# Sliding-window attention scores: five sets of exponentials per group in place of six, with quarter blocks in 32x64 tiles

## The chip, the cores and the metric

The kernel runs on one core of a Trainium2 chip. The metric is the device time of one launch in microseconds (us). A NeuronCore has a matrix engine (TensorE, called PE in the profile; its weight loads are listed apart as PEld), a vector engine (VectorE, DVE), a scalar engine (ScalarE, ACT), a general engine (GpSimd, POOL) and a queue engine for transfers (SyncE, SP). Each works through its own list of instructions in order, and they meet by semaphores. TensorE writes to PSUM; all other data here lie in SBUF.

## The reference, cut to what matters

One transformer block on a sequence of 2048 tokens with 640 channels, in bfloat16:

```python
mod = (_silu(c) @ w_mod).reshape(c.shape[0], 6, 1, -1)      # sa, ca, ga, sb, cb, gb
h = _layernorm(x) * (1 + ca) + sa
x = x + ga * attention(h, A_wqkv, A_wo)                     # 32 heads of 20 channels, window 256
h = _layernorm(x) * (1 + cb) + sb
x = x + gb * ((sigmoid(h @ w_gate) * (h @ w_up)) @ w_down)  # 640 -> 1536 -> 640
```

In the attention a query at position i sees the keys from i - 255 to i:

```python
mask = (idx[:, None] - idx[None, :] >= 0) & (idx[:, None] - idx[None, :] < W)   # W = 256
scores = jnp.where(mask, q @ k^T * Dh ** (-0.5), -1e9);  o = softmax(scores) @ v
```

## The kernel before

**Chunks, groups, blocks.** The 2048 tokens go in eight chunks `a` of 256 queries, two blocks of 128 each. For a chunk the kernel does a layer norm, transposes it, projects Q, K and V, turns Q and K so that channels lie on partitions (by transposing DMAs from the staging tile `stg`, except for chunk 0), does the attention, the output projection, the second layer norm and the gated MLP. The 32 heads form eight groups of four: heads with the same `gi` lie on partitions 0, 32, 64 and 96 (20 of 32 used), and `j` counts these four. The attention of a chunk goes in two halves `q`, each with four `gi` (called `k` in the code); such a pair (chunk, half) is called a group below.

**Scores.** A query block of a chunk touches the key blocks at the offsets -2, -1 and 0 (first block) or -1, 0 and 1 (second block), counted in blocks from the chunk's first. Per head that makes six blocks of 128 keys by 128 queries: four of them are cut by a diagonal of the window (offset -2 with the first query block, -1 with the second, 0 with the first, 1 with the second), and of each of these four one half is dead. `plan` (L931) lays these blocks in sets. A set fills one score tile `S`, four PSUM banks with 512 columns each, one bank for each `j`. The tile pool for `S` has one tile, so a set's matmuls wait until the exponential of the set before has read it. A main set holds the blocks of offsets 0 and -1 of one `k` (8 matmuls of 256 columns); an edge set holds the blocks of offsets -2 and 1 of two `k` (16 matmuls of 128 columns). A group has four main and two edge sets; chunk 0, with no keys before it, has three sets in each half. That makes 14 x 6 + 2 x 3 = 90 sets.

**A set's course.** `score_set` (L945) issues the matmuls (through `mm`, L626, with a tile position: each of the four `j` uses its own 32 rows of the array and all 128 columns), then one exponential on ScalarE from `S` to a tile `E` (L975; 128 x 2048 elements), then masks on POOL that set the dead half of each cut block to zero (`affine_select`, L983 and L985): in a main set two of 512 elements per partition, in an edge set two of 1024. There are eight `E` tiles.

**Products with V.** `burst` (L992) multiplies all `E` of a group with V: 64 matmuls, each on 32 columns of the array (`j` picks which), 32 of 256 and 32 of 128 columns. From chunk 1 on it is held in `pend` and put in front of the matmuls of the next group's second set, in one operation of TensorE. V has a column of ones, so that the sums of the softmax come out beside the products; `norm` divides (VectorE).

**Order.** Nothing is ordered at run time. `A(...)` records operations with the tiles they read and write, and `PLAN` is a written list of them all in the order of issue; an entry is five times the operation's number plus the engine's. `SLOTS` is a written list of the buffers that tiles take. `schedule` turns both into one list for each engine, and `emit` puts in the semaphore waits that the tiles call for. Between score sets the list of TensorE holds matmuls of projections and of the MLP (through the same `mm`, L625).

## Time and profile before

| what | value |
|---|---|
| time, median of 3 runs | 329.41 us (328.96 to 330.71) |
| profiled execution, first to last instruction of the program (span) | 327.1 us |
| profiled execution, time with what surrounds the program | not on the page; the median lies 2.3 us above the span |
| PE busy | 318.7 us, 97% of the span |
| ACT busy | 231.4 us, 71% |
| DVE busy | 196.7 us, 60% |
| POOL busy | 183.0 us, 56% |
| 90 exponentials (L975) | 169.0 us of ACT |
| masks (L983, L985) | 139.3 us of POOL |

Busy time is the union of an engine's instructions. A matmul's record reaches from its issue to a modelled end, so records of matmuls overlap, and the time that one costs is read from start to start. In a timeline row the first number is the start, the second how long the merged row lasts, then engine, line, operation, what it writes and reads, the shapes (stationary rows*columns, then moving rows x columns) and how many instructions the row merges. In a row of waits stand the total in us, the number of times and the longest.

### The profile page before, as it was taken

What the parts mean: (1) busy time and instruction counts of PE and PEld (TensorE: products, weight loads), DVE (VectorE), ACT (ScalarE), POOL (GpSimd) and SP (SyncE); (2) the same over time, 40 slices, a digit from 0 to 9 for tenths busy, and PEclk for the clock granted to TensorE, in tenths of its full rate; (3) what the DMA queues carried; (4) which work ended last, traced back from release to release, by engine and by line L of the source; (5) the groups of instructions that cost most, each with busy time, mean ns of one, the idle gap of its engine ahead of it and who ended that gap; (6) DMA issues with size and microseconds to landing.
All of it is one profiled execution on the core that took longest, in us unless ns stands there. A gap on an engine that the chain in (4) does not pass through costs nothing.

```text
span 327.1 us, 9812 instructions
## 1 busy us (share of the span) xinstructions
PE 318.7 (97%) x4123; PEld 227.8 (70%) x4123; DVE 196.7 (60%) x422; ACT 231.4 (71%) x227; POOL 183.0 (56%) x279
## 2 busy tenths in 40 slices
PE   5999899999999999999999999999999999999997
PEld 2666556567776777665767667766777777788885
DVE  6796799678485545675457554456727463484333
ACT  2489799987787898879797968785897568322120
POOL 4248579789688563778383745646490837402000
DMA  7989899999902281321802100360051012202101
GB/s 231 373 319 196 178 271 192 222 289 274 218 18 40 42 139 34 82 42 44 170 0 44 32 2 19 80 125 2 1 82 42 2 42 43 82 0 42 40 2 40
DMA packets 64613, 33.52 MB, mean 102 GB/s; under 512 B 49082, under 2 KB 63034, under 8 KB 64570
## 3 DMA queue, kind: packets, MB, share of 16 engines
q1 hardware_dynamic: 63200, 31.27, 42.2%
q10 hardware_dynamic: 1370, 1.64, 1.5%
q8 instruction: 32, 0.52, 0.7%
q14 instruction: 11, 0.09, 0.1%
HBM read 18.35 MB, written 2.62 MB: 64 GB/s over the span
## 4 chain that ended last, share of the span: by engine, by line
PE 93%; DMA 3%; DVE 1%; ACT 1%; issue 0%; POOL 0%; SPq 0%; DVEq 0%
PE M L625 77%; PE S L626 9%; PE M L626 7%; DMA QT<-stg 1%; DMA x<-in_A_x_dram 1%; ACT E L975 1%; DVE st L732 1%; DVE x L753 0%; SPq L524 0%; POOL st L740 0%; ACT QT L655 0%; DVE hT L814 0%; DVE st L734 0%; DVE x L1159 0%; POOL st L738 0%
## 5 line engine op out<-in xcount | busy, mean ns | idle before, releaser
L975 ACT ACTIVATE E<-S 128x2048 bf16<-128x2048 f32 x90 | 169.0, 1877 | 36.3 <-PE S L626 34.4
L983 POOL TENSOR_SCALAR_AFFINE_SELECT E<-E 128x512 bf16<-128x512 bf16 (+2 forms) x90 | 73.7, 830 | 36.2 <-ACT E L975 15.1
L985 POOL TENSOR_SCALAR_AFFINE_SELECT E<-E 128x512 bf16<-128x512 bf16 (+1 forms) x84 | 65.6, 790 | 36.4 <-ACT E L975 30.7
L625 PE MATMUL M<-h2T,wu 128*128 128x256 bf16 x480 | 73.6, 273 | 0.0
L625 PE MATMUL M<-h2T,wg 128*128 128x256 bf16 x480 | 72.7, 273 | 0.0
L1140 DVE SCALAR_TENSOR_TENSOR hh<-sig,M 128x512 bf16<-128x512 f32 x48 | 32.4, 681 | 49.5 <-ACT sig L1138 27.2
L625 PE MATMUL M<-wd,hh 128*128 128x320 bf16 (+2 forms) x396 | 60.5, 295 | 0.0
L625 PEld LDWEIGHTS M<-h2T,wu 128*128 128x128 bf16 x480 | 45.1, 98 | 10.8 <-issue 2.7
L1138 ACT ACTIVATE sig<-M 128x512 f32<-128x512 f32 x48 | 28.5, 596 | 33.5 <-PE M L625 32.4
L625 PEld LDWEIGHTS M<-h2T,wg 128*128 128x128 bf16 x480 | 45.2, 98 | 9.9 <-issue 1.9
L625 PEld LDWEIGHTS M<-wd,hh 128*128 128x128 bf16 x396 | 36.8, 98 | 14.9 <-issue 1.9
L626 PE MATMUL S<-QT,KT 20*128 20x256 bf16 (+1 forms) x960 | 35.9, 245 | 1.8 <-DMA QT<-stg 1.3
L626 PEld LDWEIGHTS S<-QT,KT 20*128 20x128 bf16 x960 | 14.1, 92 | 21.9 <-ACT E L975 11.6
L732 DVE BATCH_NORM_STATS2 st<-x 128x6 f32<-128x320 bf16 x64 | 29.0, 476 | 0.6 <-DMA x<-in_A_x_dram 0.5
L625 PE MATMUL M<-wk,hT 128*128 128x320 bf16 x160 | 29.4, 300 | 0.0
L1021 DVE STREAM_TRANSPOSE T<-M 128x512 f32<-128x512 f32 x32 | 21.6, 698 | 12.7 <-PE S L626 12.2
L625 PE MATMUL M<-wv,hT 128*128 128x320 bf16 x160 | 28.6, 300 | 0.0
L625 PE MATMUL M<-wo,oT 128*128 128x320 bf16 x160 | 28.0, 300 | 0.0
L625 PE MATMUL M<-wq,hT 128*128 128x320 bf16 x160 | 27.6, 300 | 0.3 <-DVE hT L814 0.3
L1159 DVE TENSOR_TENSOR x<-M,x 128x320 bf16<-128x320 f32 (+2 forms) x33 | 15.4, 475 | 17.9 <-PE M L625 17.6
L1094 DVE TENSOR_TENSOR x<-M,x 128x320 bf16<-128x320 f32 x32 | 15.3, 486 | 16.0 <-PE M L625 15.3
L656 DVE CAST stg<-M 128x320 bf16<-128x320 f32 x33 | 15.7, 483 | 12.5 <-PE M L625 12.4
(82 smaller groups left out, 303.2 us busy)
## 6 DMA issues: line engine op xcount, KB each, us to landing
x<-in_A_x_dram SPq DMA_DIRECT2D x10, 320.0 KB, 4.3
wd<-in_w_mod_dram SPq DMA_DIRECT2D x6, 320.0 KB, 5.1
wd<-in_B_w_down_dram SPq DMA_DIRECT2D x4, 480.0 KB, 5.0
out_dram<-x SPq DMA_DIRECT2D x4, 320.0 KB, 2.4
wg<-in_B_w_gate_dram SPq DMA_DIRECT2D x2, 576.0 KB, 7.3
wu<-in_B_w_up_dram SPq DMA_DIRECT2D x2, 576.0 KB, 5.9
wu<-in_w_mod_dram SPq DMA_DIRECT2D x1, 960.0 KB, 11.0
out_dram<-x ACTq DMA_DIRECT2D x3, 320.0 KB, 2.3
```

The costliest lines, as they stand in the source:

```text
L625: return e.matmul(o, l, r, start=st, stop=sp, skip_group_check=True)
L626: return e.matmul(o, l, r, start=st, stop=sp, tile_position=tp, skip_group_check=True)
L656: return e.tensor_copy(dst(), src())
L732: A("dve", lambda e, g, bi=bi, j=j: e.bn_stats(v(bi * 12 + j * 6, 6), src[bi].ap[:, j * 320:(j + 1) * 320]), 0.48, reads=[src[bi].r()], wr ...
L975: A("act", lambda e, eng: e.activation(E.ap[:], Sp.ap[:], ACT.Exp, scale=SM_SCALE), 1.876, reads=[Sp.r()], writes=[E.r()], prio=3, tag=f"e ...
L983: return e.affine_select(ap, ap, pattern=[[0, ap.shape[1]], [1, 128]], compare_op=ALU.is_ge, fill=0.0, base=0, channel_multiplier=-1)
L985: return e.affine_select(ap, ap, pattern=[[0, ap.shape[1]], [-1, 128]], compare_op=ALU.is_ge, fill=0.0, base=-1, channel_multiplier=1)
L1021: A("dve", lambda e, g, h=h: e.transpose(T1.ap[:, 512 * h:512 * h + 512], X[h].ap), 0.694, reads=[X[h].r()], writes=[T1.r(h)], prio=3.5, t ...
L1094: A("dve", lambda e, g, ps=ps, bi=bi, half=half: e.tensor_tensor(x1[bi].ap[:, half * 320:half * 320 + 320], ps.ap[:, 0:320], x1[bi].ap[:, ...
L1138: A("act", lambda e, g, pg=pg, sg=sg: e.activation(sg.ap[:], pg.ap[:], ACT.Tanh, scale=0.5), c_act(512), reads=[pg.r()], writes=[sg.r()], ...
L1140: A("dve", lambda e, g, pu=pu, sg=sg, f0=f0: e.scalar_tensor_tensor(out=hh.ap[:, f0:f0 + 2, :], in0=sg.ap[:].rearrange("p (a b) -> p a b", ...
L1159: A("dve", lambda e, g, ps=ps, bi=bi, c0=c0, n=n: e.tensor_tensor(x1[bi].ap[:, c0:c0 + n], ps.ap[:, 0:n], x1[bi].ap[:, c0:c0 + n], op=ALU. ...
```

## The change

The dead half of a cut block of 128 x 128 has one quarter of 64 x 64 that is dead as a whole. A cut block thus has one dead quarter, one live quarter, and two quarters cut by the diagonal. After the change the places of the two dead quarters of a main set are filled with live quarters from the blocks of offset 1 and -2 of the same `k`; what is left of these two blocks goes, 64 queries each, to one edge set per group for all four `k`. So a group has four main sets and one edge set: 14 x 5 + 2 x 3 = 76.

- A main set (`main_set`) now has 24 matmuls. Each writes 64 of the score tile's partitions, so a tile of the array is 32 rows by 64 columns, and the moving parts are 64, 64, 192, 192, 256 and 256 columns, alternating between the two halves of the partitions.
- The edge set (`edge_set`) has 32 matmuls of 64 columns on tiles of 32 rows by 128 columns. Its exponential writes to a tile `F` (4 x 4 x 256 elements per partition) with gaps in the middle of each row; two masks of 1024 elements follow.
- `spread` takes, for each main set, the two foreign quarters out of `E`, masks them and writes them to the gaps in `F` (two `affine_select` of 256 elements), and then masks the places that they leave in `E` with the block around them (two of 512). It runs once both the main set and `F` are there: for the first two main sets after the edge set, which is third of five (`ESI`), for the other two after their own exponential.
- The product with V reads the blocks of offset -1 and 0 from `E` and those of -2 and 1 from `F`: the same 64 matmuls.
- Q's layout puts the two query blocks of a head side by side (`p_QT`), so that a matmul can take any stretch of the 256 queries; the transposing DMAs write to strided rows.
- There are six `E` tiles and one `F` for the eight `E` of before. `PLAN` and `SLOTS` are written anew, for all engines.

```diff
 PLAN = [
...
+NE = 6
+NF = 1
+ESI = 2
...
-    p_QT = sbpool("QT", 3, [128, 2, NG, 128])
+    p_QT = sbpool("QT", 3, [128, NG, 2, 128])
...
-    Eall = sb("E", [128, 8, 2048])
-    p_E = Pool("E", [Eall[:, i, :].rearrange("p (j c) -> p j c", j=4) for i in range(8)])
+    Eall = sb("E", [128, NE, 2048])
+    p_E = Pool("E", [Eall[:, i, :].rearrange("p (j c) -> p j c", j=4) for i in range(NE)])
+    p_F = sbpool("F", NF, [128, 4, 4, 256])
...
+    def turned_heads(key, dst, bi):
+        return dst.ap[:, :, bi, :] if key == "q" else dst.ap[:, bi, :, :]
...
+    def queries(a, gi, c0, n):
+        return lambda j: QT[a].ap[32 * j:32 * j + DH, gi, :, :].rearrange("p b c -> p (b c)")[:, c0:c0 + n]
+
+    def select(dst, src, pattern, base, mul):
+        return lambda e, eng: e.affine_select(dst(), src(), pattern=pattern, compare_op=ALU.is_ge, fill=0.0, base=base, channel_multiplier=mul)
+
+    def score_set(a, q, si, tag, prods, low, E, dst, src):
...
+            for k, kb, p0, np_, c0, n, at in prods:
+                gi, kc = 4 * q + k, (2 * a + kb) // 2
+                rhs = queries(a, gi, c0, n)
                 for j in range(4):
-                    ins = mm(e, Sp.ap[:, j, cu * 128:(cu + n) * 128].rearrange("p (n c) -> p n c", c=128), KT[kc].ap[32 * j:32 * j + DH, kb % 2, gi, :],
-                             QT[a].ap[32 * j:32 * j + DH, u:u + n, gi, :], True, True, tp=(32 * j, 0))
+                    ins = mm(e, Sp.ap[p0:p0 + np_, j, at:at + n], KT[kc].ap[32 * j:32 * j + DH, kb % 2, gi, p0:p0 + np_], rhs(j),
+                             True, True, tp=(32 * j, p0))
...
+    def edge_set(a, q, si):
+
+        F = Tile(p_F, f"F{a}_{q}")
+        prods = []
+        for k in range(4):
+            prods += [(k, -2, 0, 128, 0, 64, 128 * k), (k, 1, 0, 128, 192, 64, 128 * k + 64)]
+        cols = lambda c0, t=F: t.ap[:].rearrange("p j k c -> p (j k) c")[:, :, c0:c0 + 64]
+        score_set(a, q, si, "edge", prods, False, F,
+                  lambda: F.ap[:].rearrange("p j k (u c) -> p (j k) u c", c=64)[:, :, 0:4:3, :],
+                  lambda s: s[:].rearrange("p j (k u c) -> p (j k) u c", u=2, c=64))
+        mask(a, 1024, select(lambda: cols(0), lambda: cols(0), [[0, 16], [-1, 64]], -1, 1), [F.r()], [F.r(-2)])
+        mask(a, 1024, select(lambda: cols(192), lambda: cols(192), [[0, 16], [1, 64]], 64, -1), [F.r()], [F.r(1)])
+        return F
+
+    def main_set(a, q, k, si):
+
+        E = Tile(p_E, f"E{a}_{q}_{k}")
+        prods = [(k, 1, 0, 64, 128, 64, 192), (k, -2, 64, 64, 64, 64, 256), (k, -1, 0, 64, 0, 192, 0), (k, 0, 64, 64, 64, 192, 320),
+                 (k, 0, 0, 64, 0, 256, 256), (k, -1, 64, 64, 0, 256, 0)]
+        score_set(a, q, si, "score", prods, True, E, lambda: E.ap[:], lambda s: s[:])
+        return E
+
+    def spread(a, q, k, E, F):
+        mask(a, 256, select(lambda: F.ap[:, :, k, 128:192], lambda: E.ap[:, :, 192:256], [[0, 4], [1, 64]], 0, -1),
+             [E.r()], [F.r((k, 1)), E.r("s1")])
+        mask(a, 256, select(lambda: F.ap[:, :, k, 64:128], lambda: E.ap[:, :, 256:320], [[0, 4], [-1, 64]], -65, 1),
+             [E.r()], [F.r((k, -2)), E.r("s2")])
+        mask(a, 512, select(lambda: E.ap[:, :, 128:256], lambda: E.ap[:, :, 128:256], [[0, 4], [-1, 128]], -1, 1),
+             [E.r(), E.r("s1")], [E.r("d")])
+        mask(a, 512, select(lambda: E.ap[:, :, 256:384], lambda: E.ap[:, :, 256:384], [[0, 4], [1, 128]], 0, -1),
+             [E.r(), E.r("s2")], [E.r("g")])
+
+    def sets(a, q):
+        if a == 0:
+            return first_sets(q)
+        F, Es = None, []
+        for si in range(5):
+            if si == ESI:
+                F = edge_set(a, q, si)
+                done = range(len(Es))
+            else:
+                Es.append(main_set(a, q, len(Es), si))
+                done = [len(Es) - 1] if F is not None else []
+            for k in done:
+                spread(a, q, k, Es[k], F)
...
+            out.append((k, -1, 0, 2, lambda j, E=E: E.ap[:, j, 0:256], rs))
+            out.append((k, 0, 0, 2, lambda j, E=E: E.ap[:, j, 256:512], rs))
+        for k in range(4):
+            out.append((k, -2, 0, 1, lambda j, k=k: F.ap[:, j, k, 0:128], [F.r(), F.r(-2), F.r((k, -2))]))
+            out.append((k, 1, 1, 1, lambda j, k=k: F.ap[:, j, k, 128:256], [F.r(), F.r(1), F.r((k, 1))]))
+        return out
```

135 lines of the change are left out of this document (59 added, 76 removed), and 214 rows, old and new, of the table PLAN.

## The prediction, made before the changed kernel was run

> **What bounds the kernel now.** I read the first part of the page and the chain that ended last, then the busy time by stretches, then who waited for whom, then the timeline around single score sets.
>
> ```profile
> span 327.1 us, 9812 instructions
> ...
> PE 318.7 (97%) x4123; PEld 227.8 (70%) x4123; DVE 196.7 (60%) x422; ACT 231.4 (71%) x227; POOL 183.0 (56%) x279
> ...
> PE 93%; DMA 3%; DVE 1%; ACT 1%; issue 0%; POOL 0%; SPq 0%; DVEq 0%
> ```
>
> ```profile
> 12.00:56.00 44.00, 42.14 (x615) 27.54 (x615) 36.55 (x89) 37.84 (x43) 28.24 (x46) 1.00 1.01 245
> 56.00:140.00 84.00, 84.00 (x1099) 58.83 (x1085) 54.29 (x119) 71.61 (x72) 61.75 (x84) 1.00 0.64 136
> 140.00:285.00 145.00, 144.98 (x1999) 104.48 (x1996) 77.60 (x152) 111.20 (x95) 85.11 (x121) 1.00 0.23 47
> 285.00:327.00 42.00, 39.78 (x356) 32.72 (x344) 19.99 (x38) 7.67 (x13) 2.57 (x5) 1.00 0.10 27
> ```
>
> The first number after each stretch is its length, the second PE's busy time. From 56 to 285 us PE has no hole (228.98 of 229.00); between 12 and 56 us it lacks 1.9 us; the granted clock is 1.00 throughout. A busy PE need not be one that streams, so I take the price of a column from long rows of matmuls:
>
> ```profile
> 275.80 0.40 PE L626 MATMUL S<-QT,KT 20*128 20x256 bf16 x8
> 276.13 2.35 PE L625 MATMUL M<-wd,hh 128*128 128x320 bf16 x16
> 278.41 0.40 PE L626 MATMUL S<-QT,KT 20*128 20x128 bf16 x16
> 278.74 1.80 PE L625 MATMUL M<-wd,hh 128*128 128x320 bf16 x12
> 280.38 0.38 PE L625 MATMUL M<-h2T,wg 128*128 128x256 bf16 x2
> ...
> 281.80 0.82 PE L625 MATMUL M<-h2T,wg 128*128 128x256 bf16 x6
> 282.45 0.82 PE L625 MATMUL M<-h2T,wu 128*128 128x256 bf16 x6
> 283.11 0.60 PE L625 MATMUL M<-h2T,wg 128*128 128x256 bf16 x4
> ```
>
> Start to start, twelve matmuls of 320 columns take 280.38 - 278.74 = 1.64 us, 0.137 us each; twelve of 256 columns take 283.11 - 281.80 = 1.31 us, 0.109 us each. That is 0.43 ns a column for both widths: in a chain the weights are loaded behind the stream. So the kernel is bound by what PE streams, plus a fixed charge at each change between kinds of work.
>
> The charge is read there too. A score set holds PE from its first matmul to that of the next chain: 276.13 - 275.80 = 0.33 us for a main set of 8 matmuls, 278.74 - 278.41 = 0.33 us for an edge set of 16. Each row tile streams 512 columns in it, 2 x 0.109 = 0.22 us; the other 0.11 us is fill and drain. Ahead of it stands another drain: the 16 matmuls from 276.13 should be through at 276.13 + 16 x 0.137 = 278.32, and the set starts at 278.41, 0.09 us later. A set thus costs PE 0.42 us.
>
> Real waits of PE are few:
>
> ```profile
> PEld S L626 <- ACT E L975: 11.6, 46, 0.4
> PEld S L626 <- issue: 8.0, 28, 1.6
> ...
> PE S L626 <- DMA QT<-stg: 1.3, 1, 1.3
> ...
> PEld M L626 <- POOL E L983: 1.2, 4, 0.3
> ```
>
> The first two are idle time of the weight loader, most of it the drains just priced, while PE's matmuls still ran; of PE itself only the 1.3 us for one transposed Q is a hole of size.
>
> **The change, part by part.** *Sets removed.* Seven chunks with two groups each go from six sets to five: 90 to 76, and all 14 that go are edge sets. They stand in PE's unbroken stream, so 14 x 0.42 = 5.9 us go from the path.
>
> *Exponentials removed.* 14 go with them:
>
> ```profile
> L975 ACT ACTIVATE E<-S 128x2048 bf16<-128x2048 f32 x90 | 169.0, 1877 | 36.3 <-PE S L626 34.4 <-POOL E L985 0.7
> ```
>
> 14 x 1.877 = 26.3 us leave ScalarE. I count nothing for it: PE has no hole from 56 us on that a faster ScalarE could close. The bounds are 0 and the 1.9 us that PE lacks before 56 us.
>
> *Main sets in 32x64 tiles.* 56 of them, now 24 matmuls each, in six groups of four (one per row tile): 64, 64, 192, 192, 256, 256 columns, alternating between the two halves of the array's columns. Each half streams 64 + 192 + 256 = 512 columns. If the halves run side by side, 0.33 us stands; if one after the other, 1024 columns take 0.44 + 0.11 = 0.55 us. The trace has four row tiles at once (the score sets) and four column tiles at once (the products with V), never both. The nearest row is the latter, where all four tiles share the array's rows as the two halves would:
>
> ```profile
> 141.19 1.33 PEld L626 LDWEIGHTS M<-E,V 128*32 128x32 bf16 x64 [0.26 <-POOL E L983]
> 141.19 1.50 PE L626 MATMUL M<-E,V 128*32 128x256 bf16 x64
> ...
> 142.63 0.12 PEld L626 LDWEIGHTS S<-QT,KT 20*128 20x128 bf16 x8
> 142.63 0.40 PE L626 MATMUL S<-QT,KT 20*128 20x256 bf16 x8
> ```
>
> From 141.19 to 142.63 is 1.44 us for 32 matmuls of 256 and 32 of 128 columns. Four at once that is 8 x 0.109 + 8 x 0.055 = 1.31 us of stream and 0.13 us of drain; one after the other it would be 5.2 us. So column tiles overlap in full, their 64 weight loads included. The Trainium skill, TensorE: Matmul & The Clock Gate, Part 3, says that a weight load overlaps matmuls in flight only where the row group differs. By that rule the halves of a main set would run in series, and the sum below would be +6.6 us in place of -4.0 (the first rival); this trace disagrees, since the 64 loads above share one row group and end within the 1.44 us.
>
> What the halves do not hide is the weight load at the start, since the first groups are only 64 columns (0.027 us) long. The nearest row is the modulation product, 64 columns against full weights each time:
>
> ```profile
> 7.77 0.45 PE L625 MATMUL S<-silubc,wd 128*128 128x64 bf16 x10
> 8.06 0.59 PE L612 MATMUL S<-E 128*128 128x512 bf16 x2
> ```
>
> Ten take 8.06 - 7.77 = 0.29 us, 0.029 us each, a load with every one; so a load fits behind a 64-column matmul. I allow one uncovered load of 0.03 us and take 0.36 us for a main set, near its lower bound of 0.33 because both nearest rows lie there: 56 x 0.03 = +1.7 us (bounds 0 and 56 x 0.22 = +12.3 us).
>
> *Edge sets.* 14 stay, each now eight groups of 64 columns against full weights: 8 x 0.029 = 0.232 us where 0.218 stood, 14 x 0.014 = +0.2 us.
>
> *Masks.* POOL's rows:
>
> ```profile
> L985 POOL TENSOR_SCALAR_AFFINE_SELECT E<-E 128x512 bf16<-128x512 bf16 x56 | 35.5, 640 | 29.2 <-ACT E L975 24.1 <-DVE x L753 2.5 <-DVE Tn L1025 2.5
> L983 POOL TENSOR_SCALAR_AFFINE_SELECT E<-E 128x512 bf16<-128x512 bf16 x56 | 35.2, 639 | 17.1 <-DVE Tn L1025 8.7 <-DVE wo L1187 3.5 <-ACT E L975 3.2
> ...
> L985 POOL TENSOR_SCALAR_AFFINE_SELECT E<-E 128x1024 bf16<-128x1024 bf16 x28 | 30.5, 1091 | 7.2 <-ACT E L975 6.5 <-ACT stg L655 0.7
> ```
>
> A group had eight masks of 512 and four of 1024 elements: 8 x 0.64 + 4 x 1.09 = 9.5 us. It will have eight of 512, eight of 256 (the same line down to 256 gives 0.41 us) and two of 1024: 10.6 us. POOL gains 14 x 1.1 = 15 us on its 183.0, all beside PE unless PV has to wait for it (a rival below). The product with V has the same 64 matmuls, with half of them from the shared edge tile: no change.
>
> *Layout, buffers, order.* Q's transposes land in strided rows. The cost is taken as zero: they are as many as before and PE waited for one of them once. If that one landed 1 us later, it would cost 1 us; if the order covers it, it gives 1.3 us. Eight exponential buffers become six and one edge tile of the size of two: the next group's two first main sets fit beside four held ones, and the edge tile is wanted only after PV has read it, which PE has passed by then. The new order I cannot cost; it can give back at most PE's 1.9 us, and its losses are the rivals.
>
> **Sum.** -5.9 + 1.7 + 0.2 = -4.0 us on a span of 327.1, so 323.1. The runs' median of 329.41 lies 2.3 us above that span, for what surrounds the program's instructions; I carry it over: 325.4 us.
>
> **The rivals.** *The column halves run in series.* For it: no row has row and column tiles at once. Against it: the PV rows. Price: +12.3 + 0.2 - 5.9 = +6.6 us, 336.0 us, slower. It decides from a main set of 0.33 + 5.7/56 = 0.43 us on.
>
> *The weight loads of 64-column tiles are not hidden.* A load's record lasts 0.097 us (the 19.9 us group below). If the third group had to wait for a whole one behind a 64-column matmul, that is 0.097 - 0.027 = 0.07 us a set more, 56 x 0.07 = 3.9 us in place of my 1.7: -1.8 us, 327.6 us; with the first load uncovered as well, no gain at all.
>
> ```profile
> L626 PEld LDWEIGHTS M<-E,V 128*32 128x32 bf16 x960 | 19.9, 97 | 4.1 <-issue 2.3 <-POOL E L983 1.2 <-POOL E L985 0.3
> ```
>
> The Trainium skill, TensorEngine Tiling (Array Packing), Restrictions and Gotchas, says that column tiling excludes the fast weight load, which speaks for this rival; the 32-column loads of PV, also column tiles, show no such cost, and no run here shows one of 64 columns.
>
> *PV waits for masks.* The edge set is third of five. When its exponential ends, POOL has two masks of 1.09 us, then four per main set for two sets, then two more main sets: 2.2 + 4 x 2.1 = 10.6 us. PV comes four sets later. At the 16.3 us between two PVs shown here,
>
> ```profile
> 141.26 1.43 PE M L626 x64
> ...
> 157.58 1.50 PE M L626 x64
> ```
>
> five sets stand 3.2 us apart, so about 4 x 3.2 - 2.2 = 10.6 us pass: no slack, and POOL has other work. Against it: POOL is 56% busy, and the order may put MLP matmuls before PV. From a wait of 4.0/14 = 0.29 us a group on, the gain is gone; 0.7 us a group is +5.8 us, 335.2 us.
>
> *Instruction fetches.* PE gets 2 x 896 = 1792 instructions more (960 score matmuls become 56 x 24 + 14 x 32 + 64 = 1856, each with its load), bunched in the sets.
>
> ```profile
> q8 instruction: 32, 0.52, 0.7%
> ```
>
> 32 packets against 8246 PE instructions is one per 258, so seven more. At 0.7% of 16 engines' 327.1 us, one takes 1.1 us. If PE stood still for the seven new ones that is 8 us; the 32 old ones left no hole after 56 us. I give that little.
>
> **How the numbers follow.** Forecast (halves overlap, loads mostly hidden): 0.62, its own range 322.0 to 327.5. An order that also closes early holes, down to 321.8: 0.05. Loads uncovered, or masks or fetches taking most of the gain, 327.7 to 331: 0.16. Halves in series: 0.10. Mask or fetch waits beyond the gain: 0.07. A change under 0.5% (1.65 us) can hardly be told from none. Faster 0.67, same 0.16, slower 0.17. The range of 321.8 to 331.5 leaves out the worse part of the slower cases and little below.
>
> **What would show it.** A main set's matmuls to the next chain: 0.34 to 0.40 us if right, 0.55 if the halves run in series. The edge set: 0.34 us. PE without holes from 56 us on, and PE's score line near 76/90 of its share of the chain. ScalarE's exponentials at 76 x 1.88 us. A PV whose loader waits for POOL by more than 0.3 us would show the mask rival; a hole in PE ahead of a score set put down to issue, the fetches. A main set over 0.43 us, or holes in PE over 4 us in sum, would make the forecast wrong.

## The result and the profile after

The changed kernel takes 334.49 us (333.88 to 335.52, 6 runs) against 329.19 (328.08 to 330.71, 6 runs) for the kernel before on the same chip: a ratio of 1.0169, 95% interval 1.0143 to 1.0194. Forecast was 325.4, faster. It is slower by 5.3 us, and lies outside the range of 321.8 to 331.5. Medians and ratios in this document leave out the few executions that lie far above the others of their kernel, one of e3 (403.51 us, at a granted clock of 0.756), one of e16 (334.30) and, beside e16 and e17, one of the kernel before.

The first part of its page, the chain that ended last and the queue of instruction fetches:

```profile
span 333.2 us, 11650 instructions
...
PE 318.2 (96%) x5018; PEld 232.5 (70%) x5019; DVE 208.6 (63%) x433; ACT 206.3 (62%) x212; POOL 198.9 (60%) x353
...
q8 instruction: 39, 0.64, 0.8%
...
PE 81%; DMA 6%; POOL 5%; DVE 4%; issue 2%; ACT 2%; SPq 0%; POOLq 0%; DVEq 0%
```

ScalarE fell by 25.1 us (231.4 to 206.3; 26.3 were worked out). POOL rose by 15.9 (183.0 to 198.9), which looks like the 15 that were worked out, but its rows of masks say otherwise:

```profile
L948 POOL TENSOR_SCALAR_AFFINE_SELECT E<-E 128x512 bf16<-128x512 bf16 x112 | 71.5, 652 | 5.1 <-DVE Tn L1092 1.5 <-DVE x L763 0.3
L948 POOL TENSOR_SCALAR_AFFINE_SELECT F<-E 128x256 bf16<-128x256 bf16 x112 | 47.0, 430 | 34.4 <-ACT E L982 17.8 <-PE S L636 5.0 <-DVE h2T L779 4.3
L948 POOL TENSOR_SCALAR_AFFINE_SELECT F<-F 128x1024 bf16<-128x1024 bf16 x28 | 33.0, 1183 | 18.9 <-ACT F L982 18.6 <-DVE x L763 0.3
```

With chunk 0's (4.6 and 4.0 us) all masks sum to 160.1 us, where the same sum in the kernel before is 140.1: 20 us more. The new order took 4 us of other work off POOL (of the modulations of hT and h2T it does 15 in place of 26). The fetches are 39, seven more, as worked out. What is new is the chain: PE's share went from 93% to 81%, and DMA, POOL, DVE and "issue" took it.

The prices of a set, in the chain of waits (start, length, piece):

```profile
89.73 0.36 PE S L636 x24
90.09 2.10 PE M L635 x17
92.19 0.34 PE S L636 x32
92.53 0.32 PE M L635 x2
```

A main set of 24 matmuls holds PE for 0.36 us and an edge set of 32 for 0.34, as forecast. So the change does what it says: matmul by matmul, start to next start, PE's work between 12 us and the last matmul is 4.0 us less than before (the last matmul ends at 324.78 us before, and 0.96 us up to it are idle by that count; after, it is 330.40 and 10.62; 323.82 - 319.78 = 4.04). The time went into PE's waits, which the view of who waits for whom lists for PE:

```profile
PE M L604 <- POOL ident L543: 2.9, 1, 2.9
PE M L635 <- DVE h2T L779: 1.9, 1, 1.9
PE M L636 <- POOL E L948: 1.8, 2, 0.9
PE M L635 <- DVE x L763: 1.7, 2, 1.2
PE M L635 <- issue: 1.2, 1, 1.2
PE M L635 <- DVE V L666: 0.8, 1, 0.8
PE M L636 <- issue: 0.7, 1, 0.7
```

The first and 1.2 us of the fourth are the start, which the kernel before has too; the other 0.5 us of the fourth stand at 12 us. The others are six waits in the middle, 1.9 + 1.8 + 1.2 + 0.8 + 0.7 = 6.4 us in all, where the kernel before had one of 1.3 us. Busy time by stretches (length, then each engine, the granted clock ahead of the last two numbers) shows a second loss:

```profile
41.00:48.00 7.00, 5.49 (x98) 3.20 (x105) 5.66 (x11) 3.90 (x5) 6.44 (x11) 0.76 0.63 180
...
81.00:89.00 8.00, 6.09 (x82) 4.53 (x74) 6.88 (x12) 4.24 (x7) 7.79 (x11) 0.79 1.12 265
...
96.00:330.00 234.00, 233.02 (x3642) 177.32 (x3641) 138.23 (x273) 137.27 (x132) 128.38 (x225) 1.00 0.22 46
```

In two stretches the granted clock was 0.76 and 0.79, where the kernel before has 1.00. A mean of 0.76 over 7 us is 3.4 us at half clock, and so is 0.79 over 8 us: 1.7 us of work lost in each. This is the execution that was profiled, with a granted clock of 0.990 in the mean; the other five have 0.994 or 0.995, which fits one such stretch, and spans of 332.1 to 333.8 us. From 96 us on PE lacks 0.98 us of 234, and that is a single wait.

The sum closes. The span grew by 333.2 - 327.1 = 6.1 us though the work fell by 4.0, so PE lost 10.1 us more than before. Waits 6.4 less the old 1.3, and half clock 3.4, are 8.5 of them; the rest, 1.6 us, is the 0.5 us at 12 us and stretches too short for the lines above. I use this number, the span less 327.1 plus the 4.0 us of work saved, for every run below and call it **PE's loss**. It comes from single executions, and those of the kernel before alone span 326.4 to 329.2 us on one chip (beside e1), so differences of a microsecond in it mean nothing. The expectations on record count holes matmul by matmul instead (1.0 before, 10.6 after). That count takes 80 short broadcast matmuls, which run four at a time, for series work and so lies some 4 us too low in every kernel alike; only its differences mean anything, and they leave out the first 12 us, in which some runs below lose 1 to 5 us.

What started each wait is seen in the timeline and in the chain. At 41.84 us (timeline of PE, POOL and DVE; idle before in brackets):

```profile
41.84 0.79 PE L636 MATMUL M<-E,V 128*32 128x256 bf16 x28 [0.80 <-POOL E L948]
43.33 0.30 PE L636 MATMUL M<-E,V 128*32 128x128 bf16 x4 [0.71 <-issue]
...
39.77 2.02 POOL L948 TENSOR_SCALAR_AFFINE_SELECT E<-E 128x2048 bf16<-128x2048 bf16 x1
41.74 1.37 POOL L948 TENSOR_SCALAR_AFFINE_SELECT F<-E 128x256 bf16<-128x256 bf16 x2
...
40.04 2.42 DVE L1092 TENSOR_TENSOR Tn<-T,Dr 128x640 bf16<-128x640 f32 x1
```

PV waited 0.80 us for a mask of 2.02 us. That mask is one of chunk 0, and the kernel before has it too (two of 2.00 us); it is its place in the order that is new. In the middle of that PV PE stood 0.71 us for no semaphore at all. Two PE stops of that length within 3 us, and the clock fell to half behind them. Beside the mask DVE's divide took 2.42 us; it ended 0.67 us after the mask (42.46 and 41.79), not far from its mean duration in the kernel before, 0.82 us. The 16 divides of each kernel, before and after (shortest, median and longest in ns):

```profile
L1025 DVE TENSOR_TENSOR Tn<-T,Dr x16: 812/819/826, 37.5 to 286.9; 128x640 bf16<-128x640 f32 x16
L1092 DVE TENSOR_TENSOR Tn<-T,Dr x16: 811/826/2425, 40.0 to 292.8; 128x640 bf16<-128x640 f32 x16
```

In the order of before only one divide runs beside a mask, for 0.07 us; in the changed kernel nine do, and six of them take 1.07 to 2.42 us.

At 83.20 us, in the chain:

```profile
75.68 4.99 DMA h2T<-x
...
80.70 1.28 DVE h2T L779 x2
81.98 0.26 DVE Dr L1090
82.24 0.82 DVE h2T L779 x2
...
83.20 5.10 PE M L635 x30
...
92.85 1.21 issue
94.06 2.13 PE M L635 x18
...
114.94 0.95 POOL E L948
```

A transposing load took 4.99 us, the modulations on DVE behind it came late, PE stood 1.91 us, and the second stretch at half clock followed. At 92.85 PE stood 1.21 us for nothing but its own next instruction. At 121.06 a PV waited 0.95 us for POOL, which had worked on its masks and layer norms without a break of over 0.1 us since 108.30. The sixth wait is 0.79 us at 36.78: DVE's copy of V stood in order behind layer-norm statistics that waited 1.7 us for a load, up to 32.29, and behind what DVE did without a pause from there. So four causes are read from the trace, the late loads from the chain alone and tested by no run: masks 1.8 us, late loads behind which DVE works in order 2.7, instructions 1.9, and half clock behind such stops 3.4.

### The profile page after: what moved, and what is told of

It is laid out like the page before. It is cut to its first block, busy times and chain, and to the rows that moved or that the text cites. A ratio compares the mean times of both kernels' runs of the same rounds, so it can differ in the third digit from the quotient of the medians.

```text
span 333.2 us, 11650 instructions
## 1 busy us (share of the span) xinstructions
PE 318.2 (96%) x5018; PEld 232.5 (70%) x5019; DVE 208.6 (63%) x433; ACT 206.3 (62%) x212; POOL 198.9 (60%) x353
## 4 chain that ended last, share of the span: by engine, by line
PE 81%; DMA 6%; POOL 5%; DVE 4%; issue 2%; ACT 2%; SPq 0%; POOLq 0%; DVEq 0%
PE M L635 66%; PE S L636 7%; PE M L636 7%; DMA x<-in_A_x_dram 3%; POOL E L948 2%; ACT E L982 2%; POOL F L948 2%; DMA h2T<-x 1%; DVE st L742 1%; DMA hT<-x 1%; DVE h2T L779 1%; PE S L635 1%; POOL st L750 0%; DVE x L1155 0%; PE S L622 0%
## 5 line engine op out<-in xcount | busy, mean ns | idle before, releaser
L982 ACT ACTIVATE E<-S 128x2048 bf16<-128x2048 f32 x62 | 116.3, 1876 | 41.4 <-PE S L636 41.0
L948 POOL TENSOR_SCALAR_AFFINE_SELECT E<-E 128x512 bf16<-128x512 bf16 (+1 forms) x118 | 80.1, 692 | 8.7 <-ACT E L982 2.5
L635 PE MATMUL M<-h2T,wg 128*128 128x256 bf16 x480 | 67.3, 277 | 1.9 <-DVE h2T L779 1.9
L948 POOL TENSOR_SCALAR_AFFINE_SELECT F<-E 128x256 bf16<-128x256 bf16 x112 | 47.0, 430 | 34.4 <-ACT E L982 17.8
L635 PE MATMUL M<-h2T,wu 128*128 128x256 bf16 x480 | 66.0, 273 | 1.2 <-issue 1.2
L635 PE MATMUL M<-wd,hh 128*128 128x320 bf16 (+2 forms) x396 | 56.5, 295 | 0.0
L948 POOL TENSOR_SCALAR_AFFINE_SELECT F<-F 128x1024 bf16<-128x1024 bf16 x28 | 33.0, 1183 | 18.9 <-ACT F L982 18.6
L636 PE MATMUL S<-QT,KT 20*64 20x64 bf16 (+5 forms) x1856 | 32.4, 230 | 0.5 <-ACT E L982 0.2
L982 ACT ACTIVATE F<-S 128x2048 bf16<-128x2048 f32 x14 | 26.3, 1877 | 9.0 <-PE S L636 8.8
L636 PEld LDWEIGHTS S<-QT,KT 20*64 20x64 bf16 (+1 forms) x1856 | 15.7, 101 | 18.1 <-ACT E L982 7.9
```

Source lines behind the costliest of these rows:

```text
L635: return e.matmul(o, l, r, start=st, stop=sp, skip_group_check=True)
L636: return e.matmul(o, l, r, start=st, stop=sp, tile_position=tp, skip_group_check=True)
L948: return lambda e, eng: e.affine_select(dst(), src(), pattern=pattern, compare_op=ALU.is_ge, fill=0.0, base=base, channel_multiplier=mul)
L982: A("act", lambda e, eng: e.activation(dst(), src(Sp.ap), ACT.Exp, scale=SM_SCALE), 1.876, reads=[Sp.r()], writes=[E.r()], prio=3, tag=f"e ...
```

## The experiments

First four questions: which cause, then whether the sets or the order carry it.

### e1: the changed sets in the order of before

The changed sets keep the places that the sets of before had, the second edge set of each group goes, and the masks stand where the old ones stood.

```diff
 PLAN = [
-    67, 72, 53, 58, 13, 43, ...
+    76, 139, 89, 63, 84, 202, ...
...
```

> The changed kernel's sets in the order of the kernel before: every operation that both kernels have stands where it stood, the fourth group of operations that a group lost (its second edge set) is left out, and the masks of the one edge set and of the first two main sets stand where those of the first edge set stood. Order theory (the sets save the 4.0 us that the prediction counts, and the new order loses 9.7 us in holes of PE): no hole over 1.5 us after 12 us, the time 4 us below the kernel before, about 325.2 us. Rival (the sets' own waits, masks through one edge tile, lose it in any order): PV waits for POOL in many groups and the time is 330 us or more.

355.02 us (354.40 to 356.70), ratio 1.0788 (1.0750 to 1.0825). The waits of PE:

```profile
PE M L632 <- POOL E L944: 9.5, 7, 2.1
PE M L631 <- issue: 4.3, 2, 2.3
```

PE's loss is 29.9 us (span 353.0). The order theory missed by 30 us, and the mark of its rival was met (330 us or more, PV waiting for POOL). In an order made for other masks, the masks alone cost more than the whole saving. The old order as it stands is no home for the new sets; it says nothing yet on whether a good one exists.

### e2: idle matmuls in the two long waits

```diff
...
+    fill(314, "O0_0x", 3)
+    fill(379, "g", 8)
```

> The changed kernel with idle matmuls in two holes of PE: three of 512 columns (0.65 us) ahead of the first product with V that waits for masks at 41.8 us, and eight (1.72 us) ahead of the MLP's first matmuls that wait for h2T at 83.2 us; their results are overwritten. They take only time that PE waits anyway. Clock theory (after a hole PE streams at half the clock for some 3.4 us, which costs 1.5 us at 44 to 47 us and 2.9 us at 84.6 to 88 us): both stretches of half clock go, the time falls by 4.4 us to about 330.1 us. Rival (the slow stretches have another cause, and only the holes count): no change, 334.5 us.

336.56 us (334.3 to 338.7), ratio 1.0218 (1.0163 to 1.0273): no gain. The stretches again:

```profile
41.00:48.00 7.00, 6.80 (x145) 4.03 (x137) 6.93 (x12) 6.31 (x6) 6.91 (x12) 1.00 0.72 186
81.00:89.00 8.00, 7.90 (x157) 6.14 (x159) 6.82 (x11) 4.55 (x7) 7.78 (x10) 1.00 1.16 300
89.00:96.00 7.00, 4.76 (x78) 3.11 (x67) 3.56 (x8) 2.73 (x3) 3.56 (x7) 0.76 0.52 50
```

Both half-clock stretches are gone, so in these two places the clock did fall because PE stood still; the 4.4 us that the theory added to it did not come. But the wait for an instruction at 93 us grew to 2.2 us (from 1.2), and now half clock follows there. A cause taken away moved its loss on: PE came 3.7 us earlier to the border of an instruction block (89.2 us for 92.9), and went on behind it only 2.6 us earlier (91.4 for 94.1).

### e3: small masks

The masks of 512 elements in the main sets' tiles are cut to 32 elements; that part of the causal masking is left out of the computation.

```diff
-        mask(a, 512, select(lambda: E.ap[:, :, 128:256], lambda: E.ap[:, :, 128:256], [[0, 4], [-1, 128]], -1, 1),
+        mask(a, 512, select(lambda: E.ap[:, :, 128:136], lambda: E.ap[:, :, 128:136], [[0, 4], [-1, 8]], -1, 1),
...
```

> The changed kernel with the two masks of 512 elements per main set cut to 32 elements, so the diagonals inside E are left unmasked (part of the computation is left out); all else, the order too, is as it was. It takes 112 x 0.45 = 50 us from POOL. Mask theory (PV waits for POOL make the loss): the holes at 41.8 and 121 us (0.9 and 1.0 us) go and others of their kind, time at most 332.5 us, and 331 if the slow stretch at 44 us goes too. Order theory: the hole of 2.0 us at 83 us and the slow stretch behind it stay, and the time stays above the kernel before (329.2 us).

334.68 us (332.70 to 336.04, three runs), ratio 1.0153 (1.0083 to 1.0222). POOL fell to 153.4 us, and:

```profile
PE M L635 <- issue: 3.1, 1, 3.1
...
PE M L636 <- POOL E L948: 0.8, 1, 0.8
```

With 45 us taken off POOL the time did not fall. The wait at 121 us went. The one at 41 us stayed, but its mask is chunk 0's, which this edit does not touch. The instruction wait again took what was won. So the changed masks alone are not the cause in the order that was shipped.

### e4: sixty more PE instructions at the start

Two of the idle matmuls of 512 columns at the start become 32 of 16 columns, about as long, so that all that follows stands 60 instructions later in PE's list.

```diff
-HEAT = (5, 1, 1, 1)
+HEAT = (3, 1, 1, 1)
...
+            for k in range(32 if n == HEAT[0] else 0):
+                ins = e.matmul(p_S.aps[0][:, 3, 0:16], Eall[:, 0, 0:128], Eall[:, 0, 128:144], start=True, stop=True)
```

> The changed kernel with 60 more instructions in PE's list during the wait for the first input (32 small idle matmuls in place of two large ones), so that every border between two fetched blocks of PE's instructions falls 60 instructions earlier in the program. Fetch theory (the holes at 42.6 and 92.9 us, 0.7 and 1.2 us, with no releaser, are waits for a block of instructions that was asked for late): these two holes vanish or move to other instructions, while the hole at 83 us stays. Rival (they belong to the work at that place): both stay at the same operations.

One run, 331.94 us; PE's loss 7.1 us (span 330.2). The instruction waits at 43 and 93 us are gone, and one of 1.4 us stands at 75 us; no stretch is at half clock, and the wait of 1.9 us at 83 went with them. Counted in the trace, the matmul behind each of these waits is PE's instruction number 960 and 2752 in the changed kernel and 2240 here: 192 plus 3, 10 and 8 times 256. In each case PE goes on 1.3 to 1.5 us after a record of the fetch queue has ended. So the list arrives in blocks of 256, and PE waits where a border falls into a bad moment. Sixty idle instructions brought this one run 2.6 us under the changed kernel's median, though its waits for masks grew to 2.8 us. Which waits an order meets hangs on where the borders happen to fall.

### e5: the edge set first

The edge set goes first of its group, and its tile is held from its own set on and not from the score chain before. The order is that of the kernel before, with the place of the dropped set left empty.

```diff
...
-ESI = 2
+ESI = 0
...
-AFTER = 1
+AFTER = 0
...
-                            extra=last["s"], mode=md, hold=[E])]
+                            extra=last["s"], mode=md, hold=[E] if low or a == 0 else [])]
```

> The changed kernel's sets once more in the order of the kernel before, but with the edge set first in its group: the product with V and the edge set stand where it stood with the second set, the four main sets where the third to sixth stood, and each main set's four masks where that set's two masks stood, so POOL never has more than one set's masks in a row. The first set's place is left empty. If the sets lose time only where their masks come bunched (eight behind the edge set, as in the first experiment and in the changed kernel), POOL's waits shrink from 9.5 us to under 2 us and the time is that of the kernel before less 4.0 us, plus fetch waits of 1 to 4 us: 325 to 329 us. If one edge tile makes PV wait in any order, it stays above 335 us.

339.77 us (338.49 to 341.25), ratio 1.0332 (1.0275 to 1.0388), loss 15.5 us. One line has most of it:

```profile
PE M L632 <- POOL E L944: 10.5, 8, 2.4
```

In the old spacing of sets, some 2.6 us apart (the median between two exponentials here), the 10.6 us of masks that the prediction added up for a group do not pass before PV, by my estimate. Here, in another kernel than the one forecast, the mask rival stands at about its price: 10.5 us over 14 groups are 0.75 us a group, where the rival had 0.7. The time is that of the second case of this run's expectation, above 335 us.

### e6: the sets of before with as many instructions as the changed ones

The kernel before, with the matmuls of its main sets cut into 64, 64 and 128 columns: 24 a set, 1792 more PE instructions, the same order.

```diff
-                for j in range(4):
...
+                for c0, c1 in ((0, 64), (64, 128), (128, 256)) if n == 2 and a else ((0, n * 128),):
+                    for j in range(4):
...
```

> The kernel before, with each matmul of a main set from chunk 1 on cut in three (64, 64 and 128 columns): 24 matmuls per main set as in the changed kernel, 1792 more PE instructions, as many as the change adds; sets, order, masks and exponentials are those of before. By the prices of the matmuls it costs some 0.01 us a set, 0.6 us in all. Fetch theory (PE's instructions are brought in blocks, each asked for while the block before runs, and denser instructions leave a late one uncovered in the DMA-heavy stretch to 100 us): at least one hole of 0.5 us or more with no releaser, between instructions that wait for nothing, and 331 us or more. Rival (the holes of the changed kernel belong to its order): no such hole, at most 330.5 us.

330.41 us (328.44 to 332.98, 10 runs), ratio 1.0037 (0.9999 to 1.0075). Its span, its fetches and its PE waits of over 0.2 us:

```profile
span 329.0 us, 11603 instructions
...
q8 instruction: 39, 0.64, 0.8%
```

```profile
PE M L594 <- DMA c_row<-in_c_dram: 2.3, 1, 2.3
PE M L625 <- DVE x L753: 1.7, 1, 1.7
PE M L626 <- POOL E L988: 0.7, 2, 0.5
```

With the same 39 fetches there is no wait for an instruction, so their number alone does not bring the waits. The records of the fetch queue show what does. In the changed kernel the fetch that cost 0.7 us begins 5.9 us after PE has crossed the border before, later than any in e6. The one that cost 1.2 us begins 3.2 us after, no later than three in e6 (3.2 to 3.7 us, at 72.9, 79.4 and 88.9 us); but PE takes 6.2 us or more through those blocks, and 4.4 us through that one, in which a product with V and two sets stand close together. It was near in e6: at 88.9 us a fetch of 1.0 us and the 1.3 us behind it leave 0.3 us. What falls into one block is the order's doing.

### e7 and e8: orders with the masks spaced

Four causes that move into each other's place suggest that none of them is the cause, and that the order has no slack. So I searched for orders in a model of this kernel's instructions, with loads up to 30% late, the clash of DVE and POOL and late blocks in it. e7 has the edge-first sets of e5, e8 the changed kernel itself; only the two tables differ. The cut shows e7 against e5.

```diff
 PLAN = [
-    76, 139, 89, 63, 84, 202, ...
+    33, 139, 228, 18, 72, 3, ...
...
```

> The edit: the edge-first kernel of the run before (the changed sets, the edge set first of its chain, each edge tile held from its own set and not from the score of the chain before) with another written order: a search of my own over a model of this kernel's instructions, in which a DVE instruction with both operands in the memory that it shares with GpSimd and a GpSimd instruction keep each other waiting, loads land 30% late, and block borders of PE's instruction list cost up to 1.3 us. The sets' work is the same to the instruction; only which engine takes a mask, a copy or a rotation, and when, differs. Theory (the sets give 4 us of PE time, and what the shipped version lost are waits of its order with no slack in it: masks, the shared port, late loads, a late instruction block, and half clock behind them): PE's holes after 12 us come under 3 us, and the time is 324 to 327 us, faster than before by 0.7 to 1.5%. Rival (the new sets need more of GpSimd and DVE than any order can hide, so holes of 8 to 10 us stay wherever they are put): 330 to 336 us, no faster than before. Rival (late instruction blocks come with any new order, whatever its slack): masks wait nowhere, but holes of 1 to 3 us at block borders stay, 327 to 331 us.

> The edit: the changed kernel itself, nothing in it different but the written order and the slots, searched with the same model as in the run beside this one, from the shipped order on. Theory (waits of the order): holes after 12 us come down from 10.6 us to 2 to 5 us, and the time is 325 to 329 us. Rival (the sets' own need of GpSimd and DVE): holes stay near 10 us, time 332 to 336 us. If this one stays near 334 us while the edge-first one falls under 327, it is the place of the edge set in the chain, and not the spacing of the masks, that matters.

e7: 335.85 us, ratio 1.0200 (1.0173 to 1.0226), loss 11.2 us. e8: 335.95, 1.0202 (1.0162 to 1.0242), loss 11.9. PE's waits in e7:

```profile
PE M L631 <- DVE x L759: 5.0, 1, 5.0
PE M L631 <- DVE T L1084: 2.9, 2, 2.7
PE M L632 <- POOL E L944: 1.6, 4, 0.8
```

The theories missed, by 9 us in e7 and 7 in e8, and both times lie in the range of the rival that puts the loss down to the sets themselves. But the masks, 10.5 us in e5, cost 1.6 us in e7. The loss of e7 stands at the start, where the search had moved first loads and layer norms, and at 47 us, where the weight scalings on DVE met two masks on POOL (three scalings in 3.17 us, two masks in 3.08). An order that a model likes is worth only what the model knows.

### e9 to e12: start and loads left alone, other seeds

As e7, but with the start (20 us in e9, 22 in e10) and all loads kept where the kernel before has them, then searched on with the durations of loads and scalings corrected by those two runs (e11, e12). Again only the tables differ (against e5).

```diff
 PLAN = [
     76, 139, 89, 63, 84, 202, ...
...
```

> The edit: the edge-first kernel again, with an order searched as in the run e7, but with everything of the first 20 us and every load left where the kernel before has it, and with loads taken as up to 1.8 us late. What e7 showed: in its order PE waited for masks 1.6 us in four waits (10.5 us in eight before the spacing), but 5.0 us went in the first 12 us, where the search had moved the loads and the first layer norms, and 4.1 us at 41 and 47 us. Theory (the waits of e7 are of its start and its loads, and the sets themselves can be spaced): holes after 12 us under 5 us, the first 12 us as in the kernel before, 324 to 328.5 us. Rival (what GpSimd and DVE must do between 35 and 100 us does not fit, whatever the order): holes over 6 us, 330 to 335 us.

> The edit: a second order from the same search as e9, from another seed, with the first 22 us left as the kernel before has them. It stands for the spread between orders that the model takes as equally good (0.8 us apart in it). Theory as for e9: 324 to 329.5 us. Rival as for e9: 330 to 335 us. If e9 and this one differ by more than 3 us, it is chance waits of one order that decide, and not the amount of work.

> The edit: the order of e9, searched further in a model mended by the runs e9 and e10: transposing loads take 4.0 to 4.9 us and weight loads 1 us more, the scalings of the weights and the divides on DVE take 0.75 to 1.0 us as they did beside GpSimd's masks. What e9 and e10 showed: PE's holes after 12 us are 6.0 and 5.3 us and the last matmul ends at 327.2 and 325.6 us, against 10.6 and 330.4 in the changed kernel; the difference of the last matmul follows the holes. Theory (the sets' 4 us are there in full, and the time is the floor of 320 us plus the holes plus about 4 us of tail and launch): holes after 12 us 3 to 4 us, last matmul 323.5 to 324.5, time 327 to 328.5 us, faster than before by 0.3 to 0.8%. Rival (what PE, DVE and GpSimd must do leaves 5 us of holes in any order): 329.5 to 331 us.

> As e11, from the order of e10 and another seed (1.3 us later in the model). Theory: holes 4 to 5 us, 328 to 329.5 us. Rival: 329.5 to 331 us, no better than e10's 330.13.

| run | time, us | ratio, interval | span | PE's loss |
|---|---|---|---|---|
| e9 | 331.26 | 1.0066 (1.0038 to 1.0095) | 329.6 | 6.5 |
| e10 | 330.13 | 1.0020 (0.9995 to 1.0045) | 328.0 | 4.9 |
| e11 | 330.56 | 1.0038 (1.0011 to 1.0065) | 329.1 | 6.0 |
| e12 | 332.18 | 1.0089 (1.0055 to 1.0123) | 329.8 | 6.7 |

All are faster than the changed kernel, by 2.3 to 4.4 us, and none beats the kernel before. PE waits of 0.2 to 2.8 us stand in other places in each; e10's largest line beside the start:

```profile
PE M L632 <- POOL E L944: 1.8, 5, 0.7
```

All four miss the theory's ranges, by 0.6 to 2.8 us; e9 to e11 lie in those of the rivals. Mending the model hurt e12 (from e10, ratio 1.0020 to 1.0089, with intervals apart); whether it helped e11 (from e9) cannot be told, since the intervals overlap. Whether 5 us are the price of these sets or of any order not tuned on the chip was still open.

### e14 and e15: the control, old sets in a shuffled order

The kernel before, its sets and its work untouched, with its order searched by the same means and as freely as e9 and e10.

```diff
 PLAN = [
-    76, 139, 89, 63, 84, 202, ...
+    139, 76, 63, 202, 89, 72, ...
...
```

> A control: the kernel before, its sets and its work unchanged, with its order shuffled by the same search as e9 and e10 (first 20 us and loads left, of 965 PE steps 423 moved against the others, 99 steps on another engine), to an order that the model takes as good as the one before (328.7 against 328.2 us). Theory A (any order that was not tuned on the chip gets 5 us of holes, whichever sets it has): holes 4 to 8 us, time 332.5 to 337 us. Theory B (the holes come of the changed sets, whose masks leave GpSimd and DVE too little room): holes 1 to 2.5 us, time 329 to 331 us.

> As e14 from another seed (406 PE steps moved, 104 on another engine, 328.5 us in the model). Theory A: holes 4 to 8 us, time 332.5 to 337 us. Theory B: holes 1 to 2.5 us, 329 to 331 us.

e14: 335.02 us (334.15 to 336.06), ratio 1.0173 (1.0140 to 1.0207). e15: 337.35 (335.95 to 339.26), 1.0243 (1.0204 to 1.0282). With no work saved, PE's loss is the span less 327.1: 333.9 and 336.8 give 6.8 and 9.7 us. e15's waits:

```profile
PE M L625 <- DVE stg L656: 1.7, 1, 1.7
PE M L625 <- DVE x L753: 1.5, 1, 1.5
PE M L625 <- DVE hT L769: 1.4, 2, 1.2
PE M L626 <- POOL E L983: 1.2, 2, 0.9
```

By the count of the expectations the holes are 6.0 and 9.2 us. This decides between the theories: e14 lies in the range of theory A and e15 0.4 us above it, both far above that of B. The old sets lose as much in these two new orders as the new ones do, to the same kinds of waits. Set against orders found in the same way, the new sets are faster: 331.26 and 330.13 us (e9, e10) against 335.02 and 337.35, 5.5 us between the means. The 4.0 us that the prediction worked out lie inside the spread of these four orders (3.8 to 7.2 us between single pairs). The pairs are not alike in all: the searches started from different orders, so the 5.5 is no measurement of the sets to a tenth.

### e13, e16, e17: tuned with durations from the chip

e13 searches e10's order on with each instruction and load as long as the run e10 showed it; e16 and e17 do the same from e13, and have two more idle matmuls ahead of the first transposes, where e13 waited 1.4 us and ran at half clock after it (ten matmuls of 64 columns took 0.55 us there, 0.29 in the kernel before).

```diff
 PLAN = [
...
-HEAT = (5, 1, 1, 1)
+HEAT = (7, 1, 1, 1)
...
```

> The order of e10 searched on at a small step, in a model that takes each instruction and each load as long as the run e10 showed it, and first loads and start free to move from 12 us on. Theory (an order with few holes exists for the changed sets, and the chip's own durations find it): holes after 12 us 2 to 4 us, last matmul 322 to 324, time 326 to 328.5 us, faster than before. Rival (5 us of holes stay in any order): 329.5 to 331 us.

> The order of e13 searched on with the durations that e13 showed (from 14 us on), and two more idle matmuls of 512 columns in PE's first batch, before the first transposes, where e13 waited 1.44 us for the first layer norm and ran at half clock after it. The rest of the work as in e5 and e7 to e13. Theory (with a few rounds of durations measured on the chip the changed sets get an order with few holes): holes after 12 us 2 to 3.5 us and 1 us less in the first 12 us, time 326 to 328.5 us, faster than before. Rival (the model is at its end: it moves holes and does not close them): 329 to 331 us.

> As e16 from another seed at a smaller step, with the same two idle matmuls. Theory: 326 to 328.5 us. Rival: 329 to 331 us.

e13: 329.76 us, ratio 1.0009 (0.9987 to 1.0031), loss 4.9. e16: 329.54, 0.9994 (0.9975 to 1.0013), loss 4.3. e17: 329.10 (327.49 to 330.80, 12 runs), 0.9979 (0.9958 to 1.0000), loss 4.2 us. e17's page and waits:

```profile
span 327.3 us, 11647 instructions
```

```profile
PE M L632 <- POOL E L944: 1.7, 3, 1.1
...
PE M L631 <- DMA wg<-in_B_w_gate_dram: 1.0, 1, 1.0
```

The medians fell a little with each round, every step within the intervals. The last is some 1.9% faster than the changed kernel (0.9979 over 1.0169, both against the kernel before on their own chip) and level with the kernel before. The theory's 326 to 328.5 was not reached, and all three lie in the range of the rival; two more rounds (e13, then e16 and e17 as two tries of the next) took PE's loss from e10's 4.9 to 4.3 and 4.2 us. That the changed sets can beat the old ones in an order tuned as far as the old one is made likely by e14 and e15 and is not shown: no run of mine is clearly faster than 329.2 us.

## Why the prediction was wrong

- **Sets removed, main sets, edge sets: right.** 0.36 and 0.34 us a set, and 4.0 us less work for PE.
- **The halves in series: did not happen.** A main set would have been 0.55 us.
- **Weight loads of 64-column tiles: hidden** but for the 0.03 us a set that the sum allowed. The rule of the Trainium skill, TensorE: Matmul & The Clock Gate, Part 3, by which a load overlaps matmuls in flight only where the row group differs, is contradicted by the 0.36 us: both halves of a main set share their row groups.
- **Exponentials: right** (25 us less on ScalarE, worth nothing by themselves).
- **Masks: the amount short by a quarter (20 us for 15), the wait half right.** The mean mask took longer than the rows of before said (0.43 us for 0.41, 1.18 for 1.09, the clash with DVE among the reasons); that POOL as a whole rose by 15.9 is luck, since other work left it. In the shipped order PV waits twice, 1.8 us in all, less than the 4.0 from which the rival decides, and only 0.95 of it for a mask of the changed sets. In e5, with the edge set first and the old spacing, the rival came true at its own price.
- **Instruction fetches: the number right (seven more), the cost a quarter.** 1.9 us in two waits instead of 8; and e6 shows that the number alone brings no wait.
- **Layout: no wait for a transposed Q** is listed in the changed kernel.
- **The order: the step that failed.** "The new order I cannot cost; it can give back at most PE's 1.9 us, and its losses are the rivals." The losses were bounded one by one, each mechanism alone against an order that was otherwise as good as the one before, and the new order itself was put at nothing. What came was 10.1 us more of loss. Four mechanisms together make 9.8 us, in place of the 1.3 us of before, and 1.6 us stay unassigned: 1.8 for masks, 1.9 for instructions, 2.7 for late loads with DVE in order behind them, and 3.4 of half clock. No rival named the half clock, and of late loads only a transposed Q was priced. Neither masks nor instructions reached the 4 us at which they would have decided alone. The control prices the step: the two searched orders of the old sets cost 6.8 and 9.7 us, the six of the new ones from e7 to e12 4.9 to 11.9. The profile of before had the sign of it, by my reading: no hole in 229 us while POOL and DVE are 56 and 60% busy, and 1.9 us of holes where loads fill the DMA engines (1.01 from 12 to 56 us), is the mark of one particular order, not of the kernel.
- **The sum.** 327.1 - 4.0 + 10.1 = 333.2 us of span. The 2.3 us between span and median became 1.3 (334.49 - 333.2). Both set a median against one profiled span; in one and the same execution it is 1.7 us here (334.89 - 333.2) and 2.0 in the kernel before (331.16 - 329.2, beside e1).
- **What would show it:** "holes in PE over 4 us in sum" was the right sign, and it is what came.

What stays open: why e10 to e17 come to rest at 4 to 5 us of loss. It may be the search, whose model misses waits of 0.5 to 1.2 us, or a rest that belongs to the 20 us of masks more on POOL. No run separates these.

## What to carry to other kernels

When one engine is busy for 97% of the span, as here, the written order can be worth more than the work that an edit saves: price an edit that comes with a new order as work saved minus the loss of an order not yet tuned, and get that loss from a control, the old work in a shuffled order. Here it was 7 to 10 us against a saving of 4. When several small causes each lose a microsecond and taking one away gains nothing, look for slack rather than for the guilty one, and tune the new order with durations measured on the chip before judging the change.

## What the runs showed of the hardware

- **Half clock after stops.** In the changed kernel PE's stops of 1.91 us (83 us) and of 0.80 and 0.71 us within 3 us (41 to 43 us) were each followed by 3.4 us at half clock; single stops of 1.21 us (93 us) and 0.95 us (121 us) were not. The length of a stop alone does not tell: after 1.30 us in e11 (90.7 us) the clock fell, after 2.78 us in e12 (38.6 us) and 3.49 us in e1 (227.7 us) it did not. The clock records of the traces order these cases. They begin and end on a grid of 3.413 us (37.547 us at full clock is 11 of these steps), and all 12 steps at full clock that half clock followed hold 1.5 to 3.3 us in which PE is idle. No step with less than 1.5 us was followed by it, every one over 1.95 us was, and between them both happen; the long stops of e12 and e1 fall across a border of the grid, as 1.69 and 1.44 us and as 1.56 and 1.92. The Trainium skill, TensorE: Matmul & The Clock Gate, Part 1, has a free-running window of about 3.4 us, idle in which the clock drops. The length and the grid agree; that about half a window idle is enough is what these traces show.
- **Instruction blocks.** In the changed kernel and in e1 to e4, six PE waits of 0.7 to 3.1 us stand at 192 plus a multiple of 256 in PE's list, before 96 us, while loads ran, and each ends 1.3 to 1.5 us after the end of a fetch record. In the changed kernel these records begin 5.9 and 3.2 us after PE had crossed the border before. One wait that looks alike, 2.3 us in e1 at 116 us, stands at no such border, and its cause is open; one of 0.5 us in e12 at 147 us stands at such a border. The Trainium skill, Runtime: NRT & Kernel Launch, Instruction fetch mechanics, has blocks of 256 instructions and calls the crossing mostly hidden; in the kernel before and in e6 it is, in the changed kernel and in e1 to e4 it is not.
- **DVE and POOL.** A divide with both operands in the memory shared with POOL took 2.42 us beside a mask of 2.02 us, ending 0.67 us after it, and 0.82 us in the mean of the kernel before. The mask side pays too: the longest mask of 512 elements, beside a divide at 84 us, took 1.21 us, where the median is 0.64. The Trainium skill, SBUF — State Buffer, Who interferes with whom, has an exclusive lock on the port that the two share; the rows agree. So the clash delays both, and the order of two engines that wait for no result of each other matters.
